# Convolution stage two in 64x64 tiles of the array, batches in the halves of the partitions

## The chip, the cores and the metric

The kernel runs on one core of a Trainium2 chip. The metric is the device time of one execution in microseconds, as the median of several runs. Everything is fp32; the array computes an fp32 matmul in two records of the trace, each with its own weight load.

## What is computed

A long convolution (by FFT) of the product of x and v with a filter made by a small network, gated by x, and behind it two mixture-of-experts layers. The change touches the convolution only.

```python
def _attn_ref(x, v, pos_emb, w1, w2):          # x, v: (2, 11456, 128)
    h_mlp = np.maximum(pos_emb @ w1, 0.0) @ w2
    h_filt = h_mlp * np.exp(-0.01 * np.arange(S))[:, None]
    u = x * v
    Uf = np.fft.rfft(u, n=2 * S, axis=1)
    Hf = np.fft.rfft(h_filt, n=2 * S, axis=0)
    y = np.fft.irfft(Uf * Hf[None], n=2 * S, axis=1)[:, :S, :]
    return x * y

# then: x -> _moe_ref (argmax over 8 experts, relu(x @ w1[e]) @ w2[e], gated) -> _moe2_ref (the same with an output gate)
```

## The kernel before, in words

The sequence is cut into 3 blocks of 60 x 64 points; a transform is done in two stages, one over 60 and one over 64 points. The 128 channels are taken in two halves, dh = 0 and 1. All the code below stands in one function, in an order that is written out by hand: each engine runs its instructions in the order of the calls. SyncE (SP) issues most loads in that order too, and an issue that waits for a buffer holds up those behind it; ScalarE issues the stores hd<-ho, vd<-wo and the first layer's wsp<-two.

- **Filter and first stage.** A loop over 16 chunks c runs h_hid (first layer of the filter network, tile ph of tag z), h_w2 (second layer and window, tiles pw of tag w) and h_mm (first stage of the filter's transform, tile pah of tag h, one buffer; DVE and ScalarE copy it to ho, and a store takes it to hd in DRAM). Between them a_units runs units of a_mm, the first stage of the signal's transform for dh 0: 24 tiles c of four units q each, 64 x 128 weight tiles (the signal) with 120 moving columns; after the fourth unit one engine copies 128x960 elements to spec. load_xv loads x and v for it, NXV buffers deep (8 in the first pass, 5 in the second), and a_mul multiplies them. Of the 96 units 72 run in the loop and 24 behind it.
- **Stage two**, for 60 pairs of frequencies n (30 for each dh). load_b loads the factors gb (by 4 ahead) and the filter's spectrum hb from hd. b_filt (tile phb, tag h) is the second stage of the filter: 4 matmuls with 64x128 tiles, and three ScalarE copies to hsb, one straight and two that swap the halves of the partitions, since real and imaginary parts stand in the two halves. b_fwd (tile pz, tag z) is the second stage of the signal: 8 matmuls with 64x128 tiles, each of the two row tiles with its own PSUM bank. The complex product of both is three DVE multiplications per frequency (pt, t1, t2: 768, 512 and 256 elements a partition) and two GpSimd additions (512 and 256). b_inv (tile pwb, tag w), for each single frequency k, is the first inverse stage: 2 matmuls with the full array and 384 columns, one ScalarE copy to wo, and for every second k a store to vd.
- **Order of stage two.** In one period m: b_fwd and b_filt (two ahead) for two n, with extras behind each, and then four b_inv of the period before. extras(n) issues load_b(n + 4), the loads of the second pass's x and v (n < 5), some constants, and from n = 4 on two steps of w_steps: this splits the first layer's expert weights in two parts (load two, ScalarE copy, DVE subtract, store to wsp). When it is drained (some 50 pairs later), extras calls lane_first(0) (two loads of 1 MB) and j_ask(4) (four pairs of loads vi and xr), ahead of the last load_b on the queue. Before n = 30 the signal's first stage for dh 1 runs as a block.
- **After it** j_inv (tile pai) does the last inverse stage with 128x64 tiles, two column tiles at a time; then routing and the experts follow, which the change leaves alone.

PSUM has 8 banks: tags z (2 buffers of 2 banks), w (2 of 1) and h (1 of 2).

Of the kernel before, what the change touches and what calls it, by code (L numbers as in the profile page):

```python
# [9 lines left out]
F32 = mybir.dt.float32  # L10
# [15 lines left out]
C = NBLK * NB * 64  # L26
# [27 lines left out]
for nm, w in WIDTH.items():  # L54
    PART[nm], MISC = (MISC, MISC + w), MISC + w
WS0, NJV, NXV = 4, 4, (8, 5)
SEGS = {}
# [7 lines left out]
def conv_moe_moe2_kernel(ctx: ExitStack, tc: tile.TileContext, a, out):  # L65
    nc = tc.nc
# [23 lines left out]
    NU = 24  # L90
# [35 lines left out]
    def h_hid(c):  # L126
        hid_t[c] = hp.tile([128, 384], F32, tag="hid", name="hid")
        pos = pos_t.pop(c)
        ph = ps.tile([128, 2, 512], F32, tag="z", name="ph")
        for jj, r in enumerate(half):  # L130
            nc.tensor.matmul(ph[:, jj, :384], w1[r], pos[r], start=True, stop=True)
        for jj, r in enumerate(half):
            nc.scalar.activation(out=hid_t[c][r], in_=ph[r, jj, :384], func=AF.Relu)

    def h_w2(c):
        hw_t[c] = hp.tile([128, CJ, 384], F32, tag="hw", name="hw", bufs=3)
        pw = [ps.tile([128, 512], F32, tag="w", name="pw") for _ in half]
        for blk in range(NBLK):
            s = slice(blk * 128, blk * 128 + 128)
            for jj, r in enumerate(half):  # L140
                nc.tensor.matmul(pw[jj][:, s], hid_t[c][r, s], w2s[r], start=True, stop=True)
        hid_t.pop(c)
        for jj in range(CJ):
            nc.vector.tensor_tensor(
                out=hw_t[c][:, jj, :].rearrange("p (e b d) -> p b e d", e=2, b=3),
                in0=pw[jj][:, :384].rearrange("p (b e d) -> p b e d", b=3, e=2),
                in1=win[:, c * CJ + jj, :].unsqueeze(2).unsqueeze(3).to_broadcast([128, 3, 2, 64]),
                op=ALU.mult,
            )

    def h_mm(c, jj):
        if jj == 0:
            ho_t[c] = hp.tile([128, 2, CJ, 384], F32, tag="ho", name="ho", bufs=3)
        ph = ps.tile([128, 2, 512], F32, tag="h", name="pah", bufs=1)
        pa = [ph[:, h] for h in range(2)]
        sub = lambda t, lo: t.rearrange("p (e b d) -> p e b d", e=2, b=3)[:, :, lo:lo + 2, :].rearrange("p e b d -> p e (b d)")
        for h, r in enumerate(half):
            nc.tensor.matmul(pa[h][:, :384], as1[r], hw_t[c][r, jj, :], start=True, stop=False)
        for h, r in enumerate(half):
            nc.tensor.matmul(sub(pa[h][:, :384], 1), as2[r], sub(hw_t[c][r, jj, :], 0), start=False, stop=True)  # L160
        for h, copy in enumerate((nc.vector.tensor_copy, nc.scalar.copy)):
            copy(out=ho_t[c][:, h, jj, :], in_=pa[h][:, :384])
        if jj == CJ - 1:
            hw_t.pop(c)
            nc.scalar.dma_start(
                out=hd.rearrange("p (h t) e c -> p h t (e c)", h=2)[:, :, c * CJ:(c + 1) * CJ, :],
                in_=ho_t.pop(c),
            )


    h_in, g_in, hs_t, p_t, wo_t = {}, {}, {}, {}, {}

# [9 lines left out]
    def b_filt(n):  # L182
        hh, g = h_in.pop(n), g_in[n]
        ph = ps.tile([128, 2, 512], F32, tag="h", name="phb", bufs=1)
        for r in range(2):
            for kk, rows in enumerate(half):
                nc.tensor.matmul(ph[:, kk, 0:192], g[rows, kk, r, :], hh[rows, r, :], start=(r == 0), stop=(r == 1))  # L187
        hs_t[n] = bp.tile([128, 2, 2, 3, 64], F32, tag="hsb", name="hsb", bufs=4)
        hf = hs_t[n].rearrange("p k c b d -> p k c (b d)")
        nc.scalar.copy(out=hf[:, :, 0], in_=ph[:, :, 0:192])  # L190
        for i in range(2):
            nc.scalar.copy(out=hf[64 * i:64 * i + 64, :, 1], in_=ph[64 - 64 * i:128 - 64 * i, :, 0:192])

    def b_fwd(n):
        kp = n % 30
        g = g_in.pop(n)
        pz = ps.tile([128, 2, 512], F32, tag="z", name="pz")
        for kk in range(2):
            for r in range(2):
                for s, rows in enumerate(half):  # L200
                    nc.tensor.matmul(  # L201
                        pz[:, s, kk * 192:kk * 192 + 192], g[rows, kk, r, :], spec[rows, 4 * kp + 2 * kk + r, :], start=(r == 0), stop=(r == 1)
                    )
        hsb = hs_t.pop(n)
        for kk in range(2):
            pt = bp.tile([128, 2, 2, 192], F32, tag="pt", name="pt", bufs=6)
            t1 = bp.tile([128, 2, 2, 128], F32, tag="t1", name="t1", bufs=2)
            t2 = bp.tile([128, 2, 2, 64], F32, tag="t2", name="t2", bufs=2)
            for j, dst in ((0, pt), (1, t1), (2, t2)):
                m = 3 - j  # L210
                nc.vector.tensor_tensor(  # L211
                    out=dst,
                    in0=pz[:, :, kk * 192:kk * 192 + m * 64].unsqueeze(1).to_broadcast([128, 2, 2, m * 64]),
                    in1=hsb[:, kk, :, j, :].unsqueeze(2).to_broadcast([128, 2, 2 * m, 64]),
                    op=ALU.mult,
                )
            nc.gpsimd.tensor_tensor(out=pt[:, :, :, 64:192], in0=pt[:, :, :, 64:192], in1=t1, op=ALU.add)  # L217
            nc.gpsimd.tensor_tensor(out=pt[:, :, :, 128:192], in0=pt[:, :, :, 128:192], in1=t2, op=ALU.add)
            p_t[2 * n + kk] = pt

    def b_inv(n):
        dh, k = divmod(n, P)
        pt = p_t.pop(n)
        pw = ps.tile([128, 512], F32, tag="w", name="pwb")
        for i in range(2):
            nc.tensor.matmul(pw[:, :C], gi[:, i, :], pt[:, i].rearrange("p s m -> p (s m)"), start=(i == 0), stop=(i == 1))  # L226
        q, kk = divmod(k, 2)
        if kk == 0:
            wo_t[dh, q] = bp.tile([128, 2, C], F32, tag="wo", name="wo", bufs=2)
        wo = wo_t[dh, q]  # L230
        nc.scalar.copy(out=wo[:, kk].rearrange("p (b s d) -> p s b d", b=3, s=2), in_=pw[:, :C].rearrange("p (s b d) -> p s b d", b=3, s=2))  # L231
        if kk == 1:
# [539 lines left out]
    with tc.manual_schedule():  # L772
# [13 lines left out]
        load_xv(0, 2)  # L786
        gi = load_const(a["gi"], [128, 2, 128], "gi", gp)

# [4 lines left out]
        def a_units(n):  # L793
            for _ in range(n):
# [3 lines left out]
                while state["mul"] < min(c + 3, NU):  # L798
                    a_mul(0, state["mul"], nc.gpsimd)
                    state["mul"] += 1  # L800
                a_mm(0, c, q, [both[c % 2]])
                state["unit"] += 1
# [4 lines left out]
        for c in range(-3, NC):  # L807
# [6 lines left out]
            if c >= 0:  # L814
                a_units(2)
            if state["load"] < NXV[0]:
# [6 lines left out]
            if c >= 0:  # L823
                a_units(3 if c % 2 else 2)

# [3 lines left out]
        for n in range(KP):  # L829
            load_b(n)  # L830
        while state["unit"] < 4 * NU:
            a_units(1)
        ap_[0].release()
# [10 lines left out]

        early_mul = 4
        b_filt(0)
        b_filt(1)
        n_pair, group4 = 60, lambda m: range(4 * m, 4 * m + 4)

        def extras(n):  # L850
# [21 lines left out]
            if n >= WS0 and jv is None and not drain(ws0, 2):  # L872
                wp.release()
                jv = tc.alloc_tile_pool(name="jv", bufs=1, reuse_waits="tile")
                lane_first(0)
                j_ask(4)

        misc = wg1 = None
        for m in range(30):
            if m == 15:  # L880
                eng = [nc.gpsimd, nc.vector, nc.gpsimd, nc.vector, nc.gpsimd]
                mul, load = early_mul, NXV[1]
                for c in range(NU):
# [3 lines left out]
                    for q in range(4):  # L887
                        a_mm(1, c, q, both if c == NU - 1 else [both[c % 3 == 2]])
                    if load < NU:
                        load_xv(1, load)  # L890
                        load += 1
                    if c == 10:
                        for k in group4(m - 1):
                            b_inv(k)
                ap_[0].release()
# [3 lines left out]
                wb = [[wb0.tile([128, 2 * F], F32R, name=f"wb0{q}") for q in range(2)]]  # L899
            for n in (2 * m, 2 * m + 1):  # L900
                b_fwd(n)
                if n + 2 < n_pair:
                    b_filt(n + 2)
                extras(n)
            if m and m != 15:
                for k in group4(m - 1):
                    b_inv(k)
        for k in group4(29):
            b_inv(k)
        view = lambda nm: misc[:, PART[nm][0]:PART[nm][1]]  # L910
# [169 lines left out]
def _consts():  # L1080
# [19 lines left out]
    gi = np.stack([np.concatenate([top, -top], 0), np.concatenate([bot, bot], 0)], 1)  # L1100
    gi = gi.reshape(128, 2, 2, Q).transpose(0, 1, 3, 2).reshape(128, 2, 128)
    h, t1 = np.arange(2)[:, None, None, None], np.arange(64)[None, :, None, None]
    j, blk = np.arange(NJ)[None, None, :, None], np.arange(NBLK)[None, None, None, :]
# [75 lines left out]
```

## Time and profile before

| | us |
|---|---|
| median of 3 runs | 1935.47 (1933.47 to 1940.45) |
| profiled execution | 1940.88 |
| its span | 1939.2 |
| TensorE busy / weight loads busy | 1742.0 / 1534.7 |
| DVE / ScalarE / GpSimd busy | 1202.7 / 963.7 / 863.2 |

The table is of the whole span. The convolution fills the first 478 us of it, routing the next 120, the experts most of the rest. Busy time is an average over stages with different limits, so the views further down are taken by stage. A matmul record of the trace includes filling and draining the array, and its successor overlaps it.

### The profile page before, as it was taken

What the parts mean: (1) busy time and instruction counts of PE and PEld (TensorE: products, weight loads), DVE (VectorE), ACT (ScalarE), POOL (GpSimd) and SP (SyncE); (2) the same over time, 40 slices, a digit from 0 to 9 for tenths busy, and PEclk for the clock granted to TensorE, in tenths of its full rate; (3) what the DMA queues carried; (4) which work ended last, traced back from release to release, by engine and by line L of the source; (5) the groups of instructions that cost most, each with busy time, mean ns of one, the idle gap of its engine ahead of it and who ended that gap; (6) DMA issues with size and microseconds to landing.
All of it is one profiled execution on the core that took longest, in us unless ns stands there. A gap on an engine that the chain in (4) does not pass through costs nothing.

```text
span 1939.2 us, 42565 instructions
## 1 busy us (share of the span) xinstructions
PE 1742.0 (90%) x13886; PEld 1534.7 (79%) x13886; DVE 1202.7 (62%) x3437; ACT 963.7 (50%) x2112; POOL 863.2 (45%) x863
## 2 busy tenths in 40 slices
PE   8889987987558988887879999999899999999997
PEld 6666665664227877777779999999799999999997
DVE  4568756874345766665657788787545555555554
ACT  4345544542114544443446566555456666666664
POOL 3258766884252455555543333323443333333333
PEclk9999999998869999998889999999899999999999
DMA  9778887884746887763458878456132241153341
GB/s 322 263 234 288 278 277 260 292 283 156 253 159 237 282 302 242 267 204 115 129 177 309 273 259 307 160 161 226 43 106 90 89 131 45 46 200 104 129 161 40
DMA packets 200547, 382.81 MB, mean 197 GB/s; under 512 B 25341, under 2 KB 117376, under 8 KB 184192
## 3 DMA queue, kind: packets, MB, share of 16 engines
q1 hardware_dynamic: 159744, 289.32, 45.4%
q10 hardware_dynamic: 21696, 52.96, 7.3%
q0 software_dynamic: 18880, 37.74, 5.6%
q8 instruction: 114, 1.87, 0.4%
q14 instruction: 113, 0.93, 0.2%
HBM read 536.98 MB, written 111.18 MB: 334 GB/s over the span
## 4 chain that ended last, share of the span: by engine, by line
PE 70%; DVE 9%; DMA 6%; issue 5%; ACT 4%; another core or an unknown queue 3%; SPq 1%; POOL 0%; ACTq 0%; POOLq 0%; DVEq 0%
PE ph L570 9%; PE ph L572 9%; PE ph L571 8%; PE pwb L226 8%; PE py L592 7%; PE py L590 7%; PE py L591 7%; PE pz L201 2%; PE pt L621 2%; PE pt L556 2%; DVE hl L576 2%; PE pai L683 2%; PE phb L187 1%; DMA vi<-vd 1%
## 5 line engine op out<-in xcount | busy, mean ns | idle before, releaser
L576 DVE SCALAR_TENSOR_TENSOR hl<-ph,hh 128x512 fp32r<-128x512 f32 x748 | 514.4, 688 | 431.9 <-ACT hh L575 356.4
L575 ACT ACTIVATE hh<-ph 128x512 fp32r<-128x512 f32 x748 | 447.8, 599 | 467.0 <-PE ph L572 288.5
L570 PE MATMUL ph<-xh,wb 128*128 128x256 f32 x1496 | 464.0, 310 | 46.1 <-DVE at L371 19.1
L571 PE MATMUL ph<-xl,wb 128*128 128x256 f32 x1496 | 423.6, 283 | 0.0
L572 PE MATMUL ph<-xh,wb 128*128 128x256 f32 x1496 | 422.3, 282 | 0.4 <-issue 0.4
L592 PE MATMUL py<-hh,wb 128*128 128x256 f32 x1496 | 420.4, 281 | 0.0
L590 PE MATMUL py<-hh,wb 128*128 128x256 f32 x1496 | 419.8, 281 | 0.6 <-issue 0.5
L591 PE MATMUL py<-hl,wb 128*128 128x256 f32 x1496 | 419.8, 281 | 0.1
L629 POOL DMA_INDIRECT out_dram<-xo,ixo x188 | 183.1, 974 | 363.9 <-ACT xo L624 309.2
L570 PEld LDWEIGHTS ph<-xh,wb 128*128 128x128 f32 x1496 | 287.6, 192 | 62.7 <-DVE at L371 27.2
L387 POOL DMA_INDIRECT reg<-xo,at x186 | 181.6, 976 | 272.8 <-ACT hh L575 113.7
L571 PEld LDWEIGHTS ph<-xl,wb 128*128 128x128 f32 x1496 | 289.2, 193 | 0.0
L572 PEld LDWEIGHTS ph<-xh,wb 128*128 128x128 f32 x1496 | 288.3, 193 | 0.9 <-issue 0.8
L591 PEld LDWEIGHTS py<-hl,wb 128*128 128x128 f32 x1496 | 286.0, 191 | 1.2 <-issue 0.9
L592 PEld LDWEIGHTS py<-hh,wb 128*128 128x128 f32 x1496 | 285.9, 191 | 0.0
L590 PEld LDWEIGHTS py<-hh,wb 128*128 128x128 f32 x1496 | 285.4, 191 | 0.4 <-issue 0.4
L387 POOL DMA_INDIRECT reg<-row,at x152 | 148.5, 977 | 179.9 <-DVE at L371 59.5
L217 POOL TENSOR_TENSOR pt<-pt,t 128x512 f32<-128x512 f32 x120 | 168.8, 1407 | 82.5 <-DVE t L211 82.1
L226 PE MATMUL pwb<-pt,gi 128*128 128x384 f32 x480 | 168.8, 504 | 5.5 <-ACT wo L231 5.5
L211 DVE TENSOR_TENSOR pt<-pz,hsb 128x768 f32<-128x768 f32 x120 | 114.2, 952 | 79.1 <-PE pz L201 48.2
L624 ACT ACTIVATE xo<-pt,xs 128x128 f32<-128x128 f32 x374 | 117.5, 366 | 75.9 <-PE pt L621 34.7
L226 PEld LDWEIGHTS pwb<-pt,gi 128*128 128x128 f32 x480 | 89.4, 194 | 73.8 <-POOL pt L217 13.1
(150 smaller groups left out, 2357.1 us busy)
## 6 DMA issues: line engine op xcount, KB each, us to landing
wb<-wsp SPq DMA_DIRECT2D x380, 1024.0 KB
vi<-vd SPq DMA_DIRECT2D x64, 384.0 KB
xs<-reg SPq DMA_DIRECT2D x187, 130.0 KB
vd<-wo ACTq DMA_DIRECT2D x60, 384.0 KB
wsp<-two ACTq DMA_DIRECT2D x32, 512.0 KB
wsp<-two SPq DMA_DIRECT2D x32, 512.0 KB
gb<-in_gf_dram SPq DMA_DIRECT2D x60, 256.0 KB
xt<-in_xu_dram SPq DMA_DIRECT2D x48, 256.0 KB
```

The costliest lines, as they stand in the source:

```text
L217: nc.gpsimd.tensor_tensor(out=pt[:, :, :, 64:192], in0=pt[:, :, :, 64:192], in1=t1, op=ALU.add)
L226: nc.tensor.matmul(pw[:, :C], gi[:, i, :], pt[:, i].rearrange("p s m -> p (s m)"), start=(i == 0), stop=(i == 1))
L387: i = nc.gpsimd.indirect_dma_start(out=reg[lay], out_offset=bass.IndirectOffsetOnAxis(ap=ix, axis=0), in_=rows, in_offset=None, bounds_che ...
L570: nc.tensor.matmul(o, wa[:, f:f + 128], xh, start=True, stop=False)
L571: nc.tensor.matmul(o, wa[:, f:f + 128], xl, start=False, stop=False)
L572: nc.tensor.matmul(o, wa[:, F + f:F + f + 128], xh, start=False, stop=True)
L575: nc.scalar.activation(out=hh, in_=ph, func=AF.Relu)
L576: nc.vector.scalar_tensor_tensor(out=hl, in0=ph, scalar=0.0, in1=hh.bitcast(F32), op0=ALU.max, op1=ALU.subtract)
L590: nc.tensor.matmul(y, wd[:, f:f + 128], hh[:, s], start=(cp == 0 and c == 0), stop=False)
L591: nc.tensor.matmul(y, wd[:, f:f + 128], hl[:, s], start=False, stop=False)
L592: nc.tensor.matmul(y, wd[:, F + f:F + f + 128], hh[:, s], start=False, stop=(cp == 3 and c == 1))
L629: i = nc.gpsimd.indirect_dma_start(out=out, out_offset=bass.IndirectOffsetOnAxis(ap=ix[:, t:t + 1], axis=0), in_=xo[:, t, 0:D], in_offset= ...
```

## The change

The factors are the same, but every matmul of stage two becomes 64x64 and has 192 moving columns. Real and imaginary parts of one batch now lie side by side in the free dimension of one half of the partitions; the other half holds the other batch, for frequency kk = 1 the other way round. So four products run in four quarters of the array. The filter needs both parts in both halves: four ScalarE copies instead of three. The inverse for one k takes 16 matmuls instead of 2, the constant gi is rearranged for it.

Tags w and h are merged into hw (2 buffers of 2 banks), which h_hid, h_w2, h_mm, b_filt and b_inv share. The order becomes one of single steps: inverse, filter one ahead, half a forward transform, inverse, the other half, product, with an inverse LB = 4 behind its forward transform. Each copy to spec is divided between ScalarE and DVE. The loop over c takes 3 units instead of 4 or 5 (48 instead of 72 in all), and the first filter stands 8 units before the end of those behind it. w_steps starts at n = 1, the second pass has 7 buffers of x and v, and j_ask(4) and lane_first(0) come at n = 56 and 57.

```diff
-WS0, NJV, NXV = 4, 4, (8, 5)
+WS0, LB, NJV, NXV = 1, 4, 4, (8, 7)
...
-        ph = ps.tile([128, 2, 512], F32, tag="z", name="ph")
+        ph = ps.tile([128, 2, 512], F32, tag="hw", name="ph")
...
-        pw = [ps.tile([128, 512], F32, tag="w", name="pw") for _ in half]
+        pw = ps.tile([128, 2, 512], F32, tag="hw", name="pw")
...
-        ph = ps.tile([128, 2, 512], F32, tag="h", name="pah", bufs=1)
+        ph = ps.tile([128, 2, 512], F32, tag="hw", name="pah")
...
     def b_filt(n):
         hh, g = h_in.pop(n), g_in[n]
-        ph = ps.tile([128, 2, 512], F32, tag="h", name="phb", bufs=1)
+        ph = ps.tile([128, 2, 512], F32, tag="hw", name="phb")
         for r in range(2):
             for kk, rows in enumerate(half):
-                nc.tensor.matmul(ph[:, kk, 0:192], g[rows, kk, r, :], hh[rows, r, :], start=(r == 0), stop=(r == 1))
-        hs_t[n] = bp.tile([128, 2, 2, 3, 64], F32, tag="hsb", name="hsb", bufs=4)
-        hf = hs_t[n].rearrange("p k c b d -> p k c (b d)")
-        nc.scalar.copy(out=hf[:, :, 0], in_=ph[:, :, 0:192])
-        for i in range(2):
-            nc.scalar.copy(out=hf[64 * i:64 * i + 64, :, 1], in_=ph[64 - 64 * i:128 - 64 * i, :, 0:192])
+                for o in half:
+                    nc.tensor.matmul(ph[o, kk, 0:192], g[rows, kk, r, o], hh[rows, r, :], start=(r == 0), stop=(r == 1))
+        hs = hs_t[n] = bp.tile([128, 2, 2, 3, 64], F32, tag="hsb", name="hsb", bufs=3)
+        for p, o in enumerate(half):
+            for to in half:
+                nc.scalar.copy(out=hs[to, :, p].rearrange("q k b d -> q k (b d)"), in_=ph[o, :, 0:192])
+
+    def b_fwd(n, p):
+        if p == 0:
+            z_t[0] = ps.tile([128, 2, 512], F32, tag="z", name="pz")
+        pz, g = z_t[0], g_in[n]
+        for r in range(2):
+            for s, rows in enumerate(half):
+                for kk in range(2):
+                    to = pz[half[s ^ kk], kk, 192 * p:192 * p + 192]
+                    nc.tensor.matmul(to, g[rows, kk, r, half[p]], spec[rows, 4 * (n % 30) + 2 * kk + r, :], start=(r == 0), stop=(r == 1))
...
     def b_inv(n):
         dh, k = divmod(n, P)
         pt = p_t.pop(n)
-        pw = ps.tile([128, 512], F32, tag="w", name="pwb")
-        for i in range(2):
-            nc.tensor.matmul(pw[:, :C], gi[:, i, :], pt[:, i].rearrange("p s m -> p (s m)"), start=(i == 0), stop=(i == 1))
+        pw = ps.tile([128, 2, 512], F32, tag="hw", name="pwb")
+        for i in range(4):
+            for h, rows in enumerate(half):
+                for o in half:
+                    nc.tensor.matmul(pw[o, h ^ (k % 2), 0:192], gi[rows, i, o], pt[rows, i // 2, i % 2, :], start=(i == 0), stop=(i == 3))
...
-                a_mm(0, c, q, [both[c % 2]])
+                a_mm(0, c, q, both)
...
-                a_units(2)
+                a_units(1)
...
-                a_units(3 if c % 2 else 2)
+                a_units(2)
...
         while state["unit"] < 4 * NU:
+            if state["unit"] == 4 * NU - 8:
+                b_filt(0)
             a_units(1)
...
-        b_filt(0)
-        b_filt(1)
...
-                lane_first(0)
-                j_ask(4)
+            if n == 56:
+                j_ask(4)
+            if n == 57:
+                lane_first(0)
...
-        for m in range(30):
-            if m == 15:
+        for n in range(n_pair + LB // 2):
+            if n == 30:
...
-                        a_mm(1, c, q, both if c == NU - 1 else [both[c % 3 == 2]])
+                        a_mm(1, c, q, both)
...
-            for n in (2 * m, 2 * m + 1):
-                b_fwd(n)
-                if n + 2 < n_pair:
-                    b_filt(n + 2)
-                extras(n)
-            if m and m != 15:
-                for k in group4(m - 1):
-                    b_inv(k)
+            k = 2 * n - LB
+            if k >= 0:
+                b_inv(k)
+            if n + 1 < n_pair:
+                b_filt(n + 1)
+            if n < n_pair:
+                b_fwd(n, 0)
+            if k >= 0:
+                b_inv(k + 1)
+            if n < n_pair:
+                b_fwd(n, 1)
+                b_mul(n)
+                extras(n)
```

The product (b_mul) is the second half of the old b_fwd; its three DVE multiplications and two GpSimd additions keep their shapes, pt has 5 buffers instead of 6.

## Rows read from the trace of the kernel before

**Rows 1.** Windows: busy us (instructions) of PE, PEld, DVE, ACT, POOL; PEclk, DMA share, GB/s.

```profile
0.00:106.00 106.00, 89.34 (x904) 67.46 (x904) 47.57 (x77) 44.15 (x80) 30.65 (x28) 1.00 0.81 284
106.00:264.00 158.00, 146.84 (x956) 102.40 (x958) 123.94 (x201) 80.48 (x166) 126.10 (x120) 0.98 0.83 273
264.00:309.00 45.00, 31.92 (x400) 26.89 (x398) 13.84 (x17) 18.02 (x22) 17.22 (x14) 0.96 0.73 251
309.00:434.00 125.00, 116.42 (x792) 81.54 (x792) 102.36 (x165) 65.35 (x134) 102.83 (x98) 1.00 0.86 286
434.00:478.00 44.00, 32.69 (x154) 21.05 (x154) 20.75 (x37) 11.47 (x24) 22.40 (x23) 0.84 0.45 144
```

**Rows 2.** Chain that ended last, steady stage two: start us, us, what (x records).

```profile
372.38 5.36 PE pwb L226 x16
377.74 1.52 PE pz L201 x16
...
412.54 5.48 PE pwb L226 x16
```

**Rows 3.** The same chain at the end of stage two.

```profile
434.10 4.88 DMA vi<-vd
439.00 5.93 DMA hb<-hd
...
447.12 7.61 PE pwb L226 x16
...
464.71 2.80 PE pz L201 x32
467.51 10.52 PE pwb L226 x32
```

**Rows 4.** Waits of PE, 106 to 478: who for whom, total us, times, longest us.

```profile
PE phb L187 <- DMA hb<-hd: 16.7, 4, 12.3
...
PE phb L187 <- ACT hsb L192: 6.2, 25, 0.2
PE pwb L226 <- ACT wo L231: 5.5, 4, 2.2
```

**Rows 5.** Lines 226 and 201, 340 to 400: duration ns min/median/max, first and last start.

```profile
L226 PE MATMUL pwb<-pt,gi x96: 486/486/590, 342.1 to 397.5; 128*128 128x384 f32 x96
...
L201 PE MATMUL pz<-spec,gb x192: 322/323/427, 339.7 to 399.9; 64*128 64x192 f32 x192
```

**Rows 6.** Timeline at 478: start us, us, engine, line, operation, shapes, records, idle before.

```profile
477.96 2.80 PE L683 MATMUL pai<-vi,ai 128*64 128x384 f32 x16
```

**Rows 7.** Timeline at 264, second pass of the forward transform.

```profile
263.74 1.86 PEld L108 LDWEIGHTS pa<-as,xt 64*128 64x128 f32 x32 [0.55 <-DVE t L211]
263.74 2.05 PE L108 MATMUL pa<-as,xt 64*128 64x120 f32 x32
```

**Rows 8.** Groups by line, 309 to 434: busy us, mean ns, idle before.

```profile
L217 POOL TENSOR_TENSOR pt<-pt,t 128x512 f32<-128x512 f32 x49 | 69.0, 1409 | 23.6 <-DVE t L211 23.4
...
L218 POOL TENSOR_TENSOR pt<-pt,t 128x256 f32<-128x256 f32 x49 | 35.7, 728 | 3.8
...
L192 ACT COPY hsb<-phb 64x384 f32<-64x384 f32 x50 | 23.7, 474 | 0.6
```

**Rows 9.** Chain of waits at the end of the filter stage.

```profile
87.31 0.57 DVE ho L162
87.91 0.49 ACT ho L162
88.44 0.92 PE pah L158 x4
...
101.86 4.28 DMA hb<-hd
```

**Rows 10.** Chain of waits in the second forward transform.

```profile
299.49 4.43 DMA vt<-in_vu_dram
```

**Rows 11.** Groups by line, 264 to 309.

```profile
L117 ACT COPY spec<-pa 128x960 f32<-128x960 f32 x16 | 15.3, 959 | 23.6 <-PE pa L108 23.6
```

More of the change, by code (lines that the diff above doesn't have):

```diff
@@ L140, in h_w2 @@
             for jj, r in enumerate(half):
-                nc.tensor.matmul(pw[jj][:, s], hid_t[c][r, s], w2s[r], start=True, stop=True)
+                nc.tensor.matmul(pw[:, jj, s], hid_t[c][r, s], w2s[r], start=True, stop=True)
         hid_t.pop(c)
@@ L145, in h_w2 @@
                 out=hw_t[c][:, jj, :].rearrange("p (e b d) -> p b e d", e=2, b=3),
-                in0=pw[jj][:, :384].rearrange("p (b e d) -> p b e d", b=3, e=2),
+                in0=pw[:, jj, :384].rearrange("p (b e d) -> p b e d", b=3, e=2),
                 in1=win[:, c * CJ + jj, :].unsqueeze(2).unsqueeze(3).to_broadcast([128, 3, 2, 64]),
@@ L168, in h_mm @@
             )
-    h_in, g_in, hs_t, p_t, wo_t = {}, {}, {}, {}, {}
+    h_in, g_in, z_t, hs_t, p_t, wo_t = {}, {}, {}, {}, {}, {}
     def load_b(n):
@@ L190, in b_filt @@
-        nc.scalar.copy(out=hf[:, :, 0], in_=ph[:, :, 0:192])
-        for i in range(2):
-            nc.scalar.copy(out=hf[64 * i:64 * i + 64, :, 1], in_=ph[64 - 64 * i:128 - 64 * i, :, 0:192])
[L194 to L197, printed above, removed]
-        for kk in range(2):
[L199 to L206, printed above, removed]
+                for o in half:
+                    nc.tensor.matmul(ph[o, kk, 0:192], g[rows, kk, r, o], hh[rows, r, :], start=(r == 0), stop=(r == 1))
@@ L207, in b_fwd, with b_mul @@
+    def b_mul(n):
+        pz, hs = z_t.pop(0), hs_t.pop(n)
+        g_in.pop(n)
+        for kk in range(2):
+            pt = bp.tile([128, 2, 2, 192], F32, tag="pt", name="pt", bufs=5)
             t1 = bp.tile([128, 2, 2, 128], F32, tag="t1", name="t1", bufs=2)
@@ L212, in b_fwd @@
                     out=dst,
-                    in0=pz[:, :, kk * 192:kk * 192 + m * 64].unsqueeze(1).to_broadcast([128, 2, 2, m * 64]),
-                    in1=hsb[:, kk, :, j, :].unsqueeze(2).to_broadcast([128, 2, 2 * m, 64]),
+                    in0=pz[:, kk, 0:384].rearrange("q (p c) -> q p c", p=2)[:, :, 0:m * 64].unsqueeze(1).to_broadcast([128, 2, 2, m * 64]),
+                    in1=hs[:, kk, :, j, :].unsqueeze(2).to_broadcast([128, 2, 2 * m, 64]),
                     op=ALU.mult,
@@ L230, in b_inv @@
         wo = wo_t[dh, q]
-        nc.scalar.copy(out=wo[:, kk].rearrange("p (b s d) -> p s b d", b=3, s=2), in_=pw[:, :C].rearrange("p (s b d) -> p s b d", b=3, s=2))
+        nc.scalar.copy(
+            out=wo[:, kk].rearrange("p (b s d) -> p s b d", b=3, s=2), in_=pw[:, :, 0:192].rearrange("p s (b d) -> p s b d", b=3)
+        )
         if kk == 1:
@@ L786, in conv_moe_moe2_kernel @@
         load_xv(0, 2)
-        gi = load_const(a["gi"], [128, 2, 128], "gi", gp)
+        gi = load_const(a["gi"], [128, 4, 128], "gi", gp)
         ok = lambda c: 0 <= c < NC
@@ L845, in conv_moe_moe2_kernel @@
         early_mul = 4
-        b_filt(0)
-        b_filt(1)
-        n_pair, group4 = 60, lambda m: range(4 * m, 4 * m + 4)
+        n_pair = 60
         def extras(n):
@@ L891, in conv_moe_moe2_kernel @@
                         load += 1
-                    if c == 10:
-                        for k in group4(m - 1):
-                            b_inv(k)
                 ap_[0].release()
@@ L899, in conv_moe_moe2_kernel @@
                 wb = [[wb0.tile([128, 2 * F], F32R, name=f"wb0{q}") for q in range(2)]]
-            for n in (2 * m, 2 * m + 1):
-                b_fwd(n)
-                if n + 2 < n_pair:
-                    b_filt(n + 2)
-                extras(n)
-            if m and m != 15:
[L906 to L909, printed above, removed]
+            k = 2 * n - LB
[10 more added lines that the diff above has]
+                b_mul(n)
+                extras(n)
         view = lambda nm: misc[:, PART[nm][0]:PART[nm][1]]
@@ L1101, in _consts @@
     gi = gi.reshape(128, 2, 2, Q).transpose(0, 1, 3, 2).reshape(128, 2, 128)
+    gi = np.tile(np.stack([gi[:64, 0], gi[64:, 1], gi[:64, 1], gi[64:, 0]], 1), (2, 1, 1))
     h, t1 = np.arange(2)[:, None, None, None], np.arange(64)[None, :, None, None]
```

## The prediction, made before the change was run

> **What bounds the kernel now.** I read the windows by stage first [rows 1]. The change touches only the first 478 us of the 1939.2 us span: the filter transform with the first half of the forward transform (0 to 106), stage two of dh 0 (106 to 264), the second forward transform (264 to 309), stage two of dh 1 (309 to 478). In stage two TensorE is busy 93% of 106:264 and of 309:434, at the full 2.4 GHz clock (granted 0.98 and 1.00). Then I read the chain of waits. In its steady part one period (two frequency pairs n, four inverses) goes from pwb at 372.38 to pwb at 412.54 four times, 10.04 us each, or 5.02 us per n, and nearly every piece of it is TensorE [rows 2]. So TensorE bounds stage two, but not by streaming alone. The rate of the array comes from two chain rows of different length: pz takes 1.52 us for 16 records and 2.80 for 32, so 16 more cost 1.28, 0.16 per pair of row tiles; pwb takes 5.36 for 16 and 10.52 for 32, so 0.3225 per record of the full array [rows 2, 3]. (An fp32 matmul shows as two records: the 8 inverse matmuls of a period are 16.) Streaming per n is then 8 x 0.16 for pz, 4 x 0.16 for phb, 8 x 0.3225 for pwb: 4.50 us. The other 0.52 per n, 1.04 per period, is what the change can reach. Part is the switch between 64x128 tiles and the full array: the longest matmul of each line, the one behind a switch or wait, is 104 ns longer than the median [rows 5]. Part is that phb has one buffer, and the next b_filt waits for three ScalarE copies: 6.2 us in 25 waits in the sequencer's waits, to which drain and refill come [rows 4].
>
> Outside the steady part the largest waits are hb loads, 16.7 us in 4, one of 12.3 [rows 4]; that one is at 439.00, where hb loads queue on SP behind lane_first and j_ask (about 4.5 MB), and the clock granted in 434:478 is 0.84 with pwb at 7.61 us instead of 5.36 [rows 1, 3].
>
> **The change, part by part.**
>
> *Streaming.* b_filt goes from 4 to 8 matmuls per n, b_fwd from 8 to 16, b_inv from 4 to 32 (two k), each 64x64 with 192 columns: 56 matmuls, 112 records. Four tiles at once make 28 slots of 0.16: 4.5 us. The array does the same work; nothing is won or lost here if four tiles really run at once. The trace has no 64x64 matmul. Nearest below: pai runs two column tiles, and its 16 records of 384 columns take 2.80 us where pwb's 16 take 5.36 [rows 2, 6], so column tiles double; pz shows that row tiles double. Both together are not shown; if only two of four ran, n would cost 4.5 more. Weight loads are no bound: the forward transform loads 32 x 128 columns in 1.86 us [rows 7], 256 columns per 0.116 us, and 64x64 tiles need the same 256 per 0.16. The rate of instructions is open: 224 per n (load and matmul) against 64 now. The fastest stretch seen is 64 in some 1.86 us, 29 ns each [rows 7]; needed are 4.5 / 224 = 20 ns. That stretch is explained by its weight columns, so it is no proven limit. I take no cost, and 29 ns as the bad end: 224 x 29 = 6.5 us per n.
>
> One rule speaks against the change. b_fwd writes bank kk from both row tiles at once, in different partition halves; before, each row tile had its own bank. pai's two tiles also write one bank in two halves at full rate, though those are column tiles [rows 6]. The Trainium skill, TensorEngine Tiling (Array Packing), section Restrictions and Gotchas, says that different row tiles cannot access the same PSUM bank simultaneously; by that the forward transforms could not overlap as written. Its PSUM page (PSUM — Partial Sum Buffer, section PSUM bank collisions raise a hardware error) narrows it to bank and quadrant, which b_fwd keeps apart.
>
> *Switches and the phb wait.* Stage two is now in one tile shape, and filter and inverse share two buffers (hw): both parts of the 0.52 us can go. What is late next? Per n the others need, from 309:434 with 24.7 n (49.3 bursts): GpSimd 102.83 / 24.7 = 4.2, DVE 102.36 / 24.7 = 4.1, DMA 0.86 x 125 / 24.7 = 4.35 [rows 1], ScalarE 65.35 / 24.7 = 2.65 plus a fourth hsb copy of 0.47 = 3.1 [rows 1, 8]. All fit under 4.5, but four resources stand within 10% of it. The lag LB = 4 gives pt of k = 2n one iteration plus nothing: the product starts 0.2 after b_fwd, DVE and GpSimd need about 3.8 (the GpSimd adds alone 1.41 + 0.73 [rows 8]), the inverse wants it 4.5 after. The margin is 0.5 us, and a late w_steps subtract or load eats it. So I take 4.8 us per n, between the floor 4.5 and today's 5.02, with both as ends.
>
> *First half of stage two*, 158 us. 30 x 4.8 less four inverses left over (4 x 1.29 = 5.2) = 138.8; filling 2.5; waits for hb and two that remain, about 7.5 (of the 16.7 + 5.5 in [rows 4], what is not the 12.3), as DMA stands at 0.83 now and must carry two more xv pairs and an earlier w_steps [rows 1]: 149. Gain 8.5, ends 0 and 16.
>
> *Second forward transform*, 45 us. It is bound by loads: the last vt lands at 303.9 [rows 10], 19 pairs in 40 us, 2.1 each. NXV 7 leaves 17: 36, plus 2 to finish, = 38. Halving the spec copy (0.96 us on one engine [rows 11]) between two engines costs nothing extra, being beside that. The leftover inverses move to the next part. Gain 7.5, ends 0 and 10.
>
> *Second half*, 169 us. 30 x 4.8 + 5.2 = 149.2; the last inverse waits for the last GpSimd add, 2.2; smaller waits 3: 154.4. Here the 12.3 us wait goes, since j_ask and lane_first now come at n = 56 and 57, behind the last load_b (n = 55). What hides them there: from n = 56 on 4.5 MB have about 27 us. If that cover is short, j_first waits instead. Gain 14.5, ends 5 and 22.
>
> *Filter stage*, 106 us. Its chain shows pah in turn with its two copies (ho 0.57 and 0.49, then pah again) [rows 9], the cost of one h buffer; two hw buffers let them overlap, but hid, pw and pah now share these two. The loop does 48 units of forward transform instead of 72, so it is shorter by 24 x 0.23 = 5.5, and those run behind it, over the wait from hd write to hb load (96 to 106, the hb load alone 4.28 [rows 9]). DMA at 0.81 on average caps it [rows 1]. Gain 6, ends 0 and 12.
>
> *What follows* (vi loads, routing, experts) starts earlier by the same amount; I take 0, ends -5 and +5.
>
> **Sum.** 8.5 + 7.5 + 14.5 + 6 = 36.5 us. The profiled execution took 1940.9 (span 1939.2), so 1904; the median of the three runs, 1935.5, lies 5.4 lower: 1935.5 - 36.5 = 1899. All good ends give 60 us, 1875; all bad ones about none.
>
> **Rivals.**
> (a) *Four tiles can't be fed.* Instructions, 224 per n, come no faster than 29 ns: 6.5 us per n, 60 x 1.7 = 102 over my 4.8, so 1899 + 102 = 2001. It turns to slower above 4.8 + 36.5 / 60 = 5.4 us per n, 24 ns an instruction. For it: that no stretch shows a faster sustained rate; against: rows 7 are filled by weight columns. Chance 0.09.
> (b) *Row tiles of b_fwd block each other in the shared bank.* Its 8 slots become 16: 1.28 x 60 = 77, so 1976. For it: no row shows two row tiles in one bank; against it: pai's halves [rows 6]. Chance 0.05. This is the case of the rule named above.
> (c) *The four-way array is no array of four*, two tiles run: 4.5 x 60 = 270 more, 2169. Chance 0.02.
> (d) *Another engine takes over*: GpSimd, DMA or the short lag keep n at 5.0 and the loads hold both forward stages where they are. Then only the moved 12.3 us wait and some filling stay, and a part returns as waits for vi: 1930. For it: the four resources at 4.1 to 4.35, and DMA shares of 0.81 to 0.86. Chance 0.10.
>
> **How the numbers follow.** The forecast has 0.72, with 1872 to 1925 as its own range. The remaining 0.02 is for dependence troubles that I do not see (slower). Faster by over 0.5% (below 1926): 0.74 with a little of (d). Within 0.5%, about what a measurement of this kernel can tell from no change: 0.09. Slower: 0.17. To leave out no more than 2 in 10 the range takes in (d) and the bad ends: 1868 to 1940.
>
> **What would show it.** Right: in steady stage two, records of four tiles starting together and 16 of 192 columns in some 0.64 us beyond the lead; a period of k by k at 4.6 to 4.9 us per n; no phb wait on hsb, no 12 us hb wait; stage two's second half near 154 us. Wrong: TensorE busy with the queue behind it (pitch over 0.16 per four records, idle put down to issue): (a) or (b, only on the b_fwd line). Idle before the inverse put down to GpSimd's add, or before b_filt to hb loads: (d). If routing after stage two grows by what stage two lost, the gain was given back.

## The result, and the profile after

The changed kernel takes 1916.3 us (median of 4 runs, 1915.7 to 1920.7) against 1936.2 for the kernel before, a ratio of 0.990 with a 95% interval of 0.9876 to 0.9924: 20 us faster, a good half of the 37 us forecast. Measured a second time, beside some of the experiments, it stands at 0.9883 (0.986 to 0.9907). The profiled execution spans 1914.0 us. Its windows, cut at the changed kernel's own stages (first b_fwd at 120, second forward transform 272 to 309, last inverse 461.5, first down product of the experts 574); columns as in [rows 1]:

```profile
0.00:120.00 120.00, 95.55 (x932) 72.13 (x934) 48.66 (x89) 46.79 (x96) 30.65 (x28) 0.94 0.75 257
120.00:272.00 152.00, 139.17 (x3216) 133.10 (x3216) 121.28 (x196) 93.00 (x192) 122.52 (x116) 0.97 0.88 290
272.00:309.00 37.00, 28.57 (x400) 26.12 (x396) 24.81 (x39) 13.75 (x26) 21.89 (x18) 0.91 0.85 293
309.00:461.50 152.50, 145.57 (x3474) 138.79 (x3468) 121.23 (x200) 93.13 (x193) 124.76 (x120) 0.99 0.83 273
461.50:574.00 112.50, 60.47 (x297) 26.94 (x298) 45.82 (x209) 19.30 (x47) 40.10 (x41) 0.73 0.60 201
574.00:1914.00 1340.00, 1257.19 (x10391) 1202.58 (x10390) 847.80 (x2736) 726.19 (x1640) 523.64 (x541) 0.98 0.52 174
```

Against the kernel before, cut at the same events (107, 264, 309, 478, 589.5):

| stage | before, us | after, us | difference | forecast |
|---|---|---|---|---|
| filter, to the first b_fwd | 107 | 120 | +13 | -6 |
| stage two, dh 0 | 157 | 152 | -5 | -8.5 |
| second forward transform | 45 | 37 | -8 | -7.5 |
| stage two, dh 1 | 169 | 152.5 | -16.5 | -14.5 |
| routing | 111.5 | 112.5 | +1 | 0 |
| experts | 1349.5 | 1340 | -9.5 | 0 |

The convolution gave 16.5 us, where 36.5 were forecast. The experts' 9.5 are in code that the change leaves alone, and the traces speak for scatter: from the first to the last down product (tile py) the trace of before has 1338.6 us, the changed kernel 1328.9, and three of its variants below, all with the same experts, 1326.5, 1330.2 and 1334.0. In the comparisons in which the experts are shorter, two variants of the kernel before have 1255.7 and 1256.0, the changed kernel 1258.0. Of the 20 us between the medians 3 to 4 are left that no stage accounts for. The one stage of the convolution that went the wrong way is the first.

TensorE in steady stage two, timeline of the changed kernel; it answers to [rows 2]:

```profile
384.23 1.55 PE L230 MATMUL pwb<-pt,gi 64*64 64x192 f32 x32
385.53 0.90 PE L188 MATMUL phb<-hb,gb 64*64 64x192 f32 x16
386.18 0.90 PE L202 MATMUL pz<-spec,gb 64*64 64x192 f32 x16
386.83 1.55 PE L230 MATMUL pwb<-pt,gi 64*64 64x192 f32 x32
388.13 0.90 PE L202 MATMUL pz<-spec,gb 64*64 64x192 f32 x16
388.78 1.55 PE L230 MATMUL pwb<-pt,gi 64*64 64x192 f32 x32
```

From start to start 32 records of the inverse take 1.30 us, 16 of the others 0.65: 0.163 per four records, the rate of four tiles at once. The same step returns after 388.78 - 384.23 = 4.55 us, which is one n (5.02 before). There is no gap between steps: each row lasts 0.25 us beyond the start of the next, at the changes of line as between two steps.

What is left are single waits. Waits of PE from 115 to 270, then what ScalarE waited for from 120 to 272:

```profile
PE pwb L230 <- ACT wo L235: 6.8, 4, 2.7
PE pz L202 <- issue: 3.3, 2, 1.9
PE pwb L230 <- POOL pt L220: 1.9, 1, 1.9
...
ACT two L270 <- DMA two<-in_m0w_dram: 7.0, 4, 4.2
```

The copy of the inverse stands behind the first step of w_steps in ScalarE's queue, that step waits for its load, and then TensorE has no free hw buffer. One such place, ScalarE's step and then TensorE's wait:

```profile
134.19 0.63 ACT L270 ACTIVATE two<-two 128x512 fp32r<-128x512 f32 x1 [4.16 <-DMA two<-in_m0w_dram]
135.33 1.19 PE L230 MATMUL pwb<-pt,gi 64*64 64x192 f32 x9 [2.66 <-ACT wo L235]
```

The median n is 4.55 in both halves, but the first half loses 20 us over that and the second 8 (sum of the excess of 28 and 29 steps).

And the filter stage. Issues on SyncE's queue, then GpSimd's product of x and v, then TensorE's forward transform:

```profile
87.84 0.42 SPq L96 DMA_DIRECT2D vt<-in_vu_dram  x1
88.31 0.42 SPq L177 DMA_DIRECT2D gb<-in_gf_dram  x1
96.07 1.33 SPq L180 DMA_DIRECT2D hb<-hd  x2
...
103.23 0.53 SPq L96 DMA_DIRECT2D xt<-in_xu_dram  x1
...
107.99 1.26 POOL L100 TENSOR_TENSOR xt<-xt,vt 128x512 f32<-128x512 f32 x1 [15.73 <-DMA vt<-in_vu_dram]
...
99.59 2.20 PE L108 MATMUL pa<-as,xt 64*128 64x120 f32 x32 [0.39 <-DVE spec L117]
109.30 5.94 PE L108 MATMUL pa<-as,xt 64*128 64x120 f32 x48 [7.51 <-POOL xt L100]
```

The first load_b stands on SyncE until the filter's last store has landed (issue at 88.31, hb at 96.07), the other three load_b follow, and the next x and v go out at 103.23. TensorE is out of signal at 101.8, waits 7.5 us, and then works its 48 records at the lower of its two clock levels (granted 0.51 in 106:115), in 5.94 us. At the upper level some 3.0 would be needed, an estimate: 32 records take 2.05 us in [rows 7], and 16 more take 8 x 0.116, by the rate of the 32.

### The profile page after: what moved, and what is told of

Its sections match the earlier page's. It is cut to its first block, busy times and chain, and to the rows that moved or that the text cites. A ratio compares the mean times of both kernels' runs of the same rounds, so it can differ in the third digit from the quotient of the medians.

```text
span 1914.0 us, 52310 instructions
## 1 busy us (share of the span) xinstructions
PE 1726.5 (90%) x18686; PEld 1599.7 (84%) x18686; DVE 1209.6 (63%) x3465; ACT 992.1 (52%) x2191; POOL 863.6 (45%) x863
## 5 line engine op out<-in xcount | busy, mean ns | idle before, releaser
L576 PE MATMUL ph<-xh,wb 128*128 128x256 f32 x1496 | 461.6, 309 | 36.5 <-DVE at L377 17.9
L230 PE MATMUL pwb<-pt,gi 64*64 64x192 f32 x3840 | 194.1, 330 | 15.2 <-ACT wo L235 7.9
L230 PEld LDWEIGHTS pwb<-pt,gi 64*64 64x64 f32 x3840 | 163.2, 135 | 23.7 <-POOL pt L220 9.8
```

Of the source, the lines that this page charges most:

```text
L230: nc.tensor.matmul(pw[o, h ^ (k % 2), 0:192], gi[rows, i, o], pt[rows, i // 2, i % 2, :], start=(i == 0), stop=(i == 3))
L576: nc.tensor.matmul(o, wa[:, f:f + 128], xh, start=True, stop=False)
```

## The experiments

The kernel before took 1834, 1832, 1937 and 1939 us in the four comparisons. By the two traces of the changed kernel the difference lies in routing (85 against 112 us) and in the experts (1258 against 1329), hardly in the convolution; what makes it is not known. So each result is a ratio to the kernel before of its own comparison, and times inside the convolution come from the traces.

**The queue, first try.** The changed kernel with load_b behind 16 more units.

```diff
-        for n in range(KP):
-            load_b(n)
         while state["unit"] < 4 * NU:
+            if state["unit"] == 4 * NU - 32:
+                for n in range(KP):
+                    load_b(n)
```

> The changed kernel with one edit: the first four load_b stand behind 16 more units of the forward transform instead of ahead of them, so the last x and v loads are issued before SyncE waits for the filter's store. Theory Q (the queue): the 13 us that the filter stage became longer are x and v loads held up behind that wait; expected is the first b_fwd at 104 to 108 us instead of 120, and 1901 to 1906 us. Rival L (the units themselves, 24 more behind the loop, and DMA): first b_fwd stays at 115 to 120, 1913 to 1918 us.

Ratio 0.9872 (0.9844 to 0.9901). First b_fwd at 116.1, just inside the rival's range, while the ratio lies between the two theories. The trace shows why: one pair of x and v is still issued behind load_b (107.76), and TensorE waits 5.2 us for it. The edit was one tile short.

**The queue, second try.** The same with `4 * NU - 28`.

> The changed kernel with the first four load_b behind 20 more units of the forward transform; behind 16 one pair of x and v loads was still left behind them, and TensorE waited 5.2 us for it. Theory Q (the queue): now no such wait stands ahead of the first b_fwd, which comes at 106 to 110 us instead of 120, and the total is 10 to 14 us under the changed kernel. Rival L (24 more units behind the loop): 115 us or later, at most 5 us gained.

Ratio 0.9853 (0.9819 to 0.9887), beside 0.9883 for the changed kernel in the same comparison: 6 us by the medians. First b_fwd at 111.8 instead of 121.1, and no wait for x and v is left. So the queue costs 9 us of this stage. Both fall short of what theory Q expected (106 to 110, and 10 to 14 us), so the queue is the larger part of the 13 us and not all of it. The intervals of the two ratios overlap, and the total can't tell 6 from 9.

**The units back in the loop.** The changed kernel with the loop of before.

```diff
-                a_units(1)
+                a_units(2)
...
-                a_units(2)
+                a_units(3 if c % 2 else 2)
```

> The changed kernel with the 72 units of the forward transform back in the loop (2, then 2 or 3 in a chunk). Theory Q: no x or v load is left behind the first load_b, so the stage ends as before or sooner, first b_fwd at 103 to 107 us, 1901 to 1906 us; the two hw buffers instead of one h alone would show as an end of the loop some us earlier. Rival S (the shared buffers hw slow the loop): the last pah comes later than the 94 us of the kernel before, and the total stays above 1912 us.

Ratio 0.9826 (0.9809 to 0.9842), which lies below the changed kernel's interval: 32 us under the kernel before, 10 to 14 under the changed one (by the ratios 0.9883 and 0.990). First b_fwd at 108.6, a little later than expected, and the last pah at 93.1 instead of 94.0 before: in this kernel the two shared buffers bring the loop next to nothing.

**One buffer or two.** The kernel before, with w and h merged into hw and nothing else.

```diff
-        pw = [ps.tile([128, 512], F32, tag="w", name="pw") for _ in half]
+        pw = ps.tile([128, 2, 512], F32, tag="hw", name="pw")
...
-        ph = ps.tile([128, 2, 512], F32, tag="h", name="phb", bufs=1)
+        ph = ps.tile([128, 2, 512], F32, tag="hw", name="phb")
...
-        pw = ps.tile([128, 512], F32, tag="w", name="pwb")
+        pw = ps.tile([128, 2, 512], F32, tag="hw", name="pwb")[:, 0]
```

> The kernel before, with tags w and h merged into hw (two buffers of two banks), all else as it was: full array for the inverse, 64x128 for the rest. It measures how much of the 1.04 us lost per period is the one buffer of phb. Theory B (the buffer is half): steady period 9.5 to 9.6 us instead of 10.04, 60 pairs save 13 to 16 us, 1920 to 1924 us. Rival M (the switch of tile shapes is nearly all): period 9.8 to 10.0, 1930 to 1936 us. Second rival: the inverse now waits for the filter's copies, 10.1 or more, over 1937 us.

Ratio 0.9948 (0.9932 to 0.9965), 9 us, between the two theories. The period is 9.84 (7.79 and 2.05 between transforms), inside the rival's range, but not for the rival's reason. TensorE in one period, and below it ScalarE's last copies out of the second filter's buffer:

```profile
369.81 0.81 PE L226 MATMUL pwb<-pt,gi 128*128 128x384 f32 x2
370.77 4.11 PE L226 MATMUL pwb<-pt,gi 128*128 128x384 f32 x12 [0.16 <-issue]
374.81 1.57 PE L201 MATMUL pz<-spec,gb 64*128 64x192 f32 x16
376.22 0.82 PE L187 MATMUL phb<-hb,gb 64*128 64x192 f32 x8
376.87 1.47 PE L201 MATMUL pz<-spec,gb 64*128 64x192 f32 x16
378.17 0.82 PE L187 MATMUL phb<-hb,gb 64*128 64x192 f32 x8
378.91 2.27 PE L226 MATMUL pwb<-pt,gi 128*128 128x384 f32 x5
...
369.71 0.96 ACT L192 COPY hsb<-phb 64x384 f32<-64x384 f32 x2
```

phb now follows pz without a gap, so its wait is gone (9 waits for hsb in 340 to 430 before, none here). In its place the second inverse stands at 370.77, 0.64 us behind its predecessor's last start instead of 0.32: its buffer still holds the filter, and ScalarE's copies out of it end at 370.67. So 0.2 us a period were won although 0.32 were newly lost. By that estimate phb's one buffer had about 0.5 of the 1.04 us, as theory B has it, and the switches the other half.

Of the 9 us little comes from stage two: from the first b_fwd to the last inverse are 371 us, as before. The filter stage became shorter. The lines of pah and pz, in the kernel before and then in this one; the two times of each are its first and its last start:

```profile
L158 PE MATMUL pah<-hw,as x128: 482/484/587, 9.8 to 94.0; 64*128 64x384 f32 x128
L201 PE MATMUL pz<-spec,gb x960: 322/323/524, 107.1 to 467.2; 64*128 64x192 f32 x192
...
L158 PE MATMUL pah<-hw,as x128: 482/484/587, 10.0 to 89.2; 64*128 64x384 f32 x128
L201 PE MATMUL pz<-spec,gb x960: 322/323/684, 102.0 to 462.9; 64*128 64x192 f32 x192
```

The last pah comes at 89.2 instead of 94.0 and the first b_fwd at 102.0 instead of 107.1 (93.7 and 107.0 in the kernel with the late asks alone, which has the old loop too). Here h_hid still takes tag z, and one engine copies to spec. So the second buffer alone is worth 5 us in the filter stage, near the 6 of the forecast, and the changed kernel loses them again in the same stage. That it pays in stage two with the new order, in which a filter lies between two inverses, fits the 4.55 but was not run by itself.

**The switch of tile shapes.** The changed kernel with b_filt alone in 64x128.

```diff
-                for o in half:
-                    nc.tensor.matmul(ph[o, kk, 0:192], g[rows, kk, r, o], hh[rows, r, :], start=(r == 0), stop=(r == 1))
+                nc.tensor.matmul(ph[:, kk, 0:192], g[rows, kk, r, :], hh[rows, r, :], start=(r == 0), stop=(r == 1))
```

> The changed kernel with b_filt alone in 64x128 tiles again (4 matmuls instead of 8, same result in the same place), so that TensorE changes the shape of its tiles twice per n. Theory T (the switch costs): each switch costs what it did before, 0.2 us and 0.1 of it the first weight load; steady n 4.9 to 5.0 us instead of 4.55, total 15 to 25 us over the changed kernel. Rival W (the 0.52 us of before was waits for buffers and copies, not the switch): 4.55 to 4.65, at most 5 us.

TensorE in its steady part:

```profile
384.00 1.48 PE L229 MATMUL pwb<-pt,gi 64*64 64x192 f32 x32
385.41 0.92 PE L187 MATMUL phb<-hb,gb 64*128 64x192 f32 x8
386.26 0.88 PE L201 MATMUL pz<-spec,gb 64*64 64x192 f32 x16
386.96 1.48 PE L229 MATMUL pwb<-pt,gi 64*64 64x192 f32 x32
388.26 0.83 PE L201 MATMUL pz<-spec,gb 64*64 64x192 f32 x16
```

From the start of the filter to the start of the next transform are 0.85 us where the changed kernel has 0.65, and the inverse ahead takes 1.41 where it takes 1.30; the transform behind takes 0.70 instead of 0.65. Together 0.36 us for two switches, and n is 4.91 in 46 of the 58 steps within the two halves: theory T in the steady part. But the ratio is 0.9925 (0.9904 to 0.9947), 7 us over the changed kernel and not 15 to 25 (the intervals of the two ratios just overlap), and from the first b_fwd to the last inverse are 351.9 us instead of 343.8. Of 60 x 0.36 = 22 us only 8 arrive. Most of the rest is saved in single waits: both halves together lie 18.5 us over their median pace, against 29.4 in the changed kernel run beside it. The step across the second forward transform is 2 us shorter as well. Which waits shrink, and why, was not followed.

**The next limit.** Half of the inverse's matmuls left out (`for i in range(2)` in b_inv), so the sum is incomplete.

> The changed kernel with half of the inverse's matmuls left out (i = 0 and 1 of four, so the sum is incomplete). TensorE then needs 20 slots of 0.16 per n, 3.3 us, and the steady time per n is that of the next limit. By the prediction's rows that is GpSimd or DMA at 4.2 to 4.4 us per n; if the next limit were far away it would be under 4 us.

The median n is 4.27 in the one profiled execution, where streaming alone would need 3.3. The window of its second half, and the longest of PE's waits in it:

```profile
309.00:433.00 124.00, 99.92 (x2172) 80.87 (x2172) 110.82 (x177) 81.75 (x174) 112.75 (x109) 1.00 0.91 306
...
PE pwb L230 <- POOL pt L220: 10.4, 24, 1.0
PE pwb L230 <- ACT wo L235: 7.2, 7, 1.6
```

DMA is at 0.91, GpSimd and DVE at 91% and 89%. With 8 of the 28 slots gone stage two, from the first b_fwd to the last inverse, goes from 343.8 to 320.7 us only, 7%. The rows of before gave this limit as 4.1 to 4.35.

**The late asks alone.** The kernel before, with j_ask(4) at n = 56 and lane_first(0) at n = 57.

> The kernel before, with j_ask(4) at n = 56 and lane_first(0) at n = 57 as in the changed kernel, nothing else. Theory of the prediction: the one wait of 12.3 us for hb goes and with it the half clock around 440; 1922 to 1926 us, stage two ends at 463 to 466 instead of 478. Rival G (given back): the later vi loads make the start of routing wait as much; 1932 to 1937 us.

Ratio 0.9916 (0.9889 to 0.9943), 15 us with 5 either way: the forecast of this term holds and is not given back. Its window over the place where the wait stood, to be held against the last row of [rows 1]:

```profile
430.00:470.00 40.00, 38.46 (x216) 24.92 (x216) 28.21 (x50) 17.13 (x37) 29.12 (x30) 1.00 0.69 248
```

TensorE is busy 38.5 of 40 us at the full clock, and the last inverse ends at 468.2 instead of 478.0, a little later than the 463 to 466 expected. The second half is 12.5 us shorter, about the wait of 12.3 us. The second forward transform ahead of it is some 3 us longer in this trace, so the convolution ends 9.8 us sooner; whether the 15 hold more than that, the interval can't tell.

**Two tiles ahead.** The kernel with the units in the loop, with the loads of w_steps one tile earlier, and its last store one step later. The second edit is for a wait at n = 50 of the changed kernel: two store issues stood on ScalarE's queue from 403.02 on for 4.53 us, the last waiting for the DVE subtract, and the copy of the inverse came at 407.64.

```diff
-        ws0, jv, asked_early = w_steps(0, wp, 1), None, False
+        ws0, jv, asked_early = w_steps(0, wp, 2), None, False
...
+            if i == len(todo):
+                yield
             if i:
                 store(i - 1)
```

> The changed kernel with the 72 units back in the loop, and two edits against the waits that are left in stage two: the loads of w_steps run two tiles ahead instead of one, and its last store is issued one step later, so that ScalarE does not stand for it ahead of a copy of the inverse (TensorE lost some 5 us there at n = 50). Theory D (ScalarE waits for loads that come too late, and one tile ahead is too short): the pairs of 6 to 9 us in the first half become fewer and the one at n = 50 goes, 5 to 12 us under the changed kernel with the units in the loop alone, 0.976 to 0.980 of the kernel before. Rival F (the DMA engines are full, so a load asked for earlier only pushes back another): the pair at n = 50 goes, the rest stays, 0 to 5 us, 0.980 to 0.983.

Ratio 0.9827 (0.9801 to 0.9853), the same as without. The step at n = 50 is 4.55 instead of 9.61, but the first half lies 18 us over its median pace, against 15 without the edit, now in part at other n. PE's waits from 100 to 260:

```profile
PE pwb L230 <- ACT wo L235: 4.5, 3, 3.0
PE pwb L230 <- POOL pt L220: 4.2, 4, 1.9
PE phb L188 <- issue: 3.2, 2, 2.5
```

The result is rival F's. That full DMA engines are the reason (DMA share 0.89 in 108:260), so that one load asked for earlier pushes back another, is not shown.

**Buffers and copies in the filter stage.** Two kernels on top of that: the tile of h_hid from tag z again, and then also one engine for a copy to spec in the first pass.

```diff
-        ph = ps.tile([128, 2, 512], F32, tag="hw", name="ph")
+        ph = ps.tile([128, 2, 512], F32, tag="z", name="ph")
...
-                a_mm(0, c, q, both)
+                a_mm(0, c, q, [both[c % 2]])
```

> The kernel with the units in the loop and two tiles ahead, and one edit more: the tile ph of h_hid is taken from tag z again, as before the change, so hw serves only h_w2 and h_mm in the filter stage. Theory S (hid takes the second buffer, and pah waits for its own last copies: 8 us in 15 waits in 20 to 90, none where hid stayed in z): the last pah comes at 88 to 90 us instead of 93, the first b_fwd at 103 to 106 instead of 108 to 111; 3 to 6 us, 0.979 to 0.981 of the kernel before. Rival R (the waits only change place, to the signal's copies in z, or hd and hb in DRAM set the start): last pah 89 but first b_fwd unchanged, or last pah 93 again; 0.982 to 0.984.

> The same with the copies to spec in the first pass on one engine in turn, as before the change, instead of half on each. If halving a copy is worth something where TensorE waits for the buffer z, this is 1 to 5 us slower than the same kernel with halves; the prediction took it as worth nothing beside the loads: within 2 us.

PE's waits from 20 to 90: first with h_hid in hw (the kernel of the last experiment), then with it in z, then with whole copies too.

```profile
PE pah L158 <- ACT ho L162: 8.0, 15, 1.5
```

```profile
PE ph L131 <- DVE spec L117: 3.1, 6, 0.5
PE pah L158 <- ACT ho L162: 2.6, 4, 0.8
PE pa L108 <- ACT hid L133: 2.5, 2, 1.2
```

```profile
PE pa L108 <- ACT hid L133: 2.6, 2, 1.3
PE ph L131 <- DVE spec L117: 1.0, 3, 0.3
PE ph L131 <- ACT spec L117: 0.7, 3, 0.2
```

The transforms of the last two, whose first start is the first b_fwd:

```profile
L202 PE MATMUL pz<-spec,gb x1920: 319/323/580, 110.2 to 440.9; 64*64 64x192 f32 x192
...
L202 PE MATMUL pz<-spec,gb x1920: 322/323/524, 102.0 to 433.0; 64*64 64x192 f32 x192
```

The first edit only moves the waits: last pah at 93.4 (93.2 without), first b_fwd at 110.2 (111.0). That is rival R; with the units in the loop, hid in hw is not what holds it. The second edit takes most of them away: last pah at 88.5, first b_fwd at 102.0, 8 us sooner in the trace and as early as with two buffers alone in the kernel before. So with hid in z, halving the copy in this loop costs time in the trace, where no difference or a gain was expected. That both engines then stand in TensorE's way for each tile, since they also share the copies of ho, fits the waits but was not tested, and whole copies with hid in hw were not run. The totals are 0.9821 (0.977 to 0.9873) and 0.9805 (0.9747 to 0.9862); 2 us between the medians, and the intervals overlap, so the gain of the last step is seen in the trace and not in the time.

## Why the prediction was right, and where it was not

**Direction and range** were right: 1916 against 1899 in a range of 1868 to 1940. The main mechanism was too: of the 0.52 us per n above streaming, which I put down to switches and one buffer (about half each, by the experiment with two buffers), 0.47 went (5.02 to 4.55); the other 0.05 are the pace, 0.163 instead of 0.16 in each of 28 slots. But in the convolution only 16.5 of 36.5 us came. That the total still lies in the range is owed to a range wide enough for rival (d) and the bad ends, and so in part to luck. In two places the gain that I put into the sum does not follow from the working: 158 less 148.8 is 9.2 and not 8.5, and 45 less 38 is 7 and not 7.5. Together that changes the sum by 0.2 us.

**Four tiles.** Four 64x64 tiles run at once at the rate worked out, 0.163 per four records. Rivals (a), (b) and (c) fall with that one row: 224 instructions come in 4.55 us, 20 ns each, where 29 was the fastest shown; b_fwd with two row tiles in one bank has the same 0.65 as b_filt, where each row tile has its own. So the rule that the Trainium skill gives in TensorEngine Tiling (Array Packing), section Restrictions and Gotchas, is not borne out as it stands there: row tiles in one bank ran together here, in different halves of the partitions.

**The steady n**, 4.8, was mis-sized: 4.55. The margin of 0.5 us between pt and the inverse held, and GpSimd, DVE and DMA, at 4.1 to 4.35 of 4.55 us, did not slow the median step, so rival (d) did not come about. What is lost is lost in single steps that are up to 5 us longer, 20 us in the first half, where I had 7.5 for waits beside the 30 x 0.25. So the halves come out near their forecasts (152 against 149, 152.5 against 154.4), with another division. The experiment with the filter in 64x128 points the same way from the other side: of 22 us on the steps 8 came in the time.

**The filter stage** is the step that failed, and with it the missing 17 us. I took the 24 units behind the loop as cover for the wait from hd to hb, at a gain of 6 with ends 0 and 12; the stage became 13 longer, outside these ends. Two things were wrong in it. The units issue loads (the last x and v), and these stand on SyncE's queue behind the load_b that wait for hd: 9 us by the second try. I listed the units' TensorE time and not their DMA issues, though SyncE's waits in the trace of before, from 0 to 480, have one of 10.6 us at hb for hd:

```profile
SPq L180 <- DMA hd<-ho: 10.6, 1, 10.6
```

And the gain of the two hw buffers is lost in the changed kernel. That they let pah overlap its copies was right: alone in the kernel before they bring the last pah to 89.2 and the first b_fwd to 102.0, 5 us sooner. But with halved copies the last pah comes at 93.1 to 93.4 under the old division of units, whether hid is in hw or in z, against 94.0 before. With whole copies and hid in z it comes at 88.5, and the first b_fwd 8 us sooner. Halving the copies I had costed at nothing, and only for the second pass.

**The loads in the second transform** (8 against 7.5) **and the late asks** (the wait of 12.3 gone; alone 12.5 us in the second half and 15 in the time) were as forecast; nothing was given back in routing (+1).

**Not settled:** which loads make the first half's waits. Two tiles ahead moved them without making them fewer, which speaks for full DMA engines (0.88 to 0.89 there), but no run took load from them. Nor is it settled what remains of the filter stage: 111.8 us without the queue's wait, 102.0 with the units in the loop, hid in z and whole copies.

**A version that beats both:** the changed kernel with the units back in the loop, 0.9826 (0.9809 to 0.9842), is 10 to 14 us under it. With whole copies, hid in z, the loads of w_steps two tiles ahead and the last store moved the median is lower still (0.9805), but the intervals overlap, and the time does not show that it is better.

## What to carry to other kernels

Work that is moved takes its DMA issues along: before it is counted as cover for a wait, look on which queue its loads stand, and behind whose wait. A fixed cost per step, taken from the median step, is not yet the time that its removal saves, since single waits elsewhere in the stage may shrink when the steps grow. Here 0.36 us per step were 22 us on paper and 8 in the time. And what a merged buffer is worth hangs on the order around it: in stage two of the kernel before it turned one wait into another, while in the filter stage it paid at once.

## What the runs showed of the hardware

Changing the tile shape between 64x64 and 64x128 costs 0.18 us each time (0.36 for two in the experiment). That is of the same size as between 64x128 and the full array in the kernel before: there the chain has 5.36 us for 16 records of the inverse, of which 16 x 0.3225 = 5.16 are streaming, so 0.2 [rows 2]. TensorE took 224 instructions (weight loads and matmuls of 64x64 tiles) in 4.55 us, for nine such steps in a row in the second trace of the changed kernel. Two row tiles wrote one PSUM bank, in different halves of the partitions, at 0.65 us for 16 records, the time of two row tiles with a bank each. A wait of 7.5 us on TensorE was followed by work at half the clock: 48 records in 5.94 us, granted 0.51.
